# Tokens routed into two expert regions on chip, in place of every expert over all tokens

## The chip, the cores and the metric

One core of a Trainium2 chip runs the kernel. Its engines work side by side, each through its own queue in program order: TensorE (PE in the profile, its weight loads PEld), VectorE (DVE), ScalarE (ACT), GpSimd (POOL) and SyncE (SP), the last only to issue transfers. The metric is the device time of one execution in microseconds.

## The reference

Linear attention over 8 batches, 8 heads, 576 positions and head size 64, followed by a mixture of experts over the 4608 tokens of 512 numbers that come out of it. Each token goes to one of eight experts (512 to 1024 to 512); a bias that depends on the token's modality (0 or 1) is added to the router's logits.

```python
q_s = np.exp(q - q.max(-1));  q_s /= q_s.sum(-1) + 1e-09      # softmax over the 64 numbers of a head
k_s = np.exp(k - k.max(2));   k_s /= k_s.sum(2) + 1e-09       # softmax over the 576 positions
kv  = np.einsum('bhsd,bhse->bhde', k_s, v)
x   = np.einsum('bhsd,bhde->bhse', q_s, kv)                   # to 4608 x 512
logits = x @ w_gate + modality_bias[modality_id]
e_idx  = np.argmax(logits, axis=1);  gate_w = softmax(logits)[arange(N), e_idx]
for e in range(E):
    mask = e_idx == e
    out[mask] = gate_w[mask, None] * (np.maximum(x[mask] @ w1[e], 0.0) @ w2[e])
```

On the inputs as the reference draws them, routing gives 2277 tokens to one expert, 2331 to another and none to the other six; the two are those with the largest bias of modality 0 and of modality 1.

## The kernel before, in words

Attention runs in four rounds of two batches (`bp`). A round loads q, k and v (`q_m`, `k_m`, `v_mb` for the first 512 positions, `q_t`, `k_t`, `v_tb` for the last 64), exponentiates on ACT, divides q by its sums on POOL (L198), and builds `kv_ps` on PE (L222 with a column of ones, L230, for the sums of k). A normalised `kvn` gives, after a transpose (L258, copied by L260), the router's matrix `gmat`; q is transposed on PE (L277, copied by L285 into `qt_all`), from which come the logits (L293) and the attention output (L304, L320), copied to `xt_nat`: all 4608 tokens, bf16, with the 512 numbers on the partitions.

Then the routing, over all tokens at once (L346 to L421): the largest logit per token as a mask `eq_all`, the gate `gate_all`, and a list `r_ints` of those experts that have any token, with their number.

Then the FFN. `run_slot` loads the weights of one listed expert (L470, L483; cast to bf16 by POOL and DVE, L479, L492), and `expert_pass` runs it over all 36 tiles of 128 tokens, nine blocks of 512: L510 is the first layer, L520 and L524 the relu, L531 the second layer. L539 and L547 multiply by mask and gate and add into `y_tot`. The first expert runs always, the second under a condition on the number of experts, others in a loop of L581 that counts up to that number. Behind the loop, 40 transfers on POOL write `y_tot`, cast to f32 (L586).

A tile framework sets the order of instructions on each engine when the kernel is built, from the order of the code and priorities; on the chip each queue runs in that order, with semaphores between them.

Of the kernel before, what the change touches and what calls it, by code (L numbers as in the profile page):

```python
# [13 lines left out]
I32 = mybir.dt.int32  # L14
# [18 lines left out]
def kernel(  # L33
# [13 lines left out]
    P = 128  # L47

# [17 lines left out]

    mod_i32_all = _dram_bitcast(moe_modality_id, I32)

    const_pool = ctx.enter_context(tc.tile_pool(name="const", bufs=1))
    persist_pool = ctx.enter_context(tc.tile_pool(name="persist", bufs=1))  # L70

    ident = const_pool.tile([P, P], BF16)
    make_identity(nc, ident)

    ones_bf = const_pool.tile([P, P], BF16)
    nc.vector.memset(ones_bf, 1.0)

    wg_f32 = const_pool.tile([P, KD, E], FP32)
    nc.sync.dma_start(out=wg_f32, in_=moe_w_gate.rearrange("(kp p) e -> p kp e", p=P))
    wg_sb = const_pool.tile([P, KD, E], BF16)  # L80
    nc.vector.tensor_copy(out=wg_sb, in_=wg_f32)

    bias0 = const_pool.tile([P, E], FP32)
    bias1 = const_pool.tile([P, E], FP32)
    nc.sync.dma_start(out=bias0, in_=moe_modality_bias[0:1, :].to_broadcast([P, E]))
    nc.sync.dma_start(out=bias1, in_=moe_modality_bias[1:2, :].to_broadcast([P, E]))
    biasd = const_pool.tile([P, E], FP32)
    nc.vector.tensor_sub(out=biasd, in0=bias1, in1=bias0)


    mod_i32 = const_pool.tile([P, NBP, CPB, 2], I32)
    for bp in range(NBP):
        for bl in range(2):
            base = 2 * (1152 * bp + 576 * bl)
            nc.sync.dma_start(
                out=mod_i32[:, bp, 4 * bl : 4 * bl + 4, :],
                in_=bass.AP(tensor=mod_i32_all.tensor, offset=base, ap=[[8, P], [2, JW], [1, 2]]),
            )
        nc.sync.dma_start(
            out=mod_i32[0:64, bp, 8, :],  # L100
            in_=bass.AP(tensor=mod_i32_all.tensor, offset=2 * (1152 * bp + SMAIN), ap=[[2, 64], [1, 2]]),
        )
        nc.sync.dma_start(
            out=mod_i32[64:128, bp, 8, :],
            in_=bass.AP(tensor=mod_i32_all.tensor, offset=2 * (1152 * bp + 576 + SMAIN), ap=[[2, 64], [1, 2]]),
        )
    mod_f32 = const_pool.tile([P, NBP * CPB], FP32)
    nc.vector.tensor_copy(out=mod_f32, in_=mod_i32[:, :, :, 0].rearrange("p a b -> p (a b)"))

    xtn_pool = ctx.enter_context(tc.tile_pool(name="xtn", bufs=1, side="right"))  # L110
    xt_nat = xtn_pool.tile([P, KD, N], BF16)
    logits_all = persist_pool.tile([P, NT, E], FP32)

    r_ints = persist_pool.tile([1, 4 * E], I32)
    gate_all = persist_pool.tile([P, NT], FP32)
    eq_all = persist_pool.tile([P, NT, E], BF16)

    with (
        tc.tile_pool(name="qkv_stage", bufs=1) as stage_pool,
        tc.tile_pool(name="attn_sb", bufs=2) as asb_pool,  # L120
        tc.tile_pool(name="attn_small", bufs=2) as asm_pool,
        tc.tile_pool(name="kv_ps", bufs=2, space=bass.MemoryType.PSUM) as kvps_pool,
        tc.tile_pool(name="qt_ps", bufs=2, space=bass.MemoryType.PSUM) as qtps_pool,
        tc.tile_pool(name="x_ps", bufs=2, space=bass.MemoryType.PSUM) as xps_pool,
        tc.tile_pool(name="lg_ps", bufs=1, space=bass.MemoryType.PSUM) as lgps_pool,
        tc.tile_pool(name="tmp_ps", bufs=1, space=bass.MemoryType.PSUM) as tmpps_pool,
    ):
        for bp in range(NBP):
            b0 = 2 * bp
            q_m = stage_pool.tile([P, 2, H, JW, Dh], FP32, name="q_m")  # L130
            q_t = stage_pool.tile([P, H, Dh], FP32, name="q_t")
            k_m = stage_pool.tile([P, 2, H, JW, Dh], FP32, name="k_m")
            k_t = stage_pool.tile([P, H, Dh], FP32, name="k_t")

            def load_main(dst, src_t, b, bl, eng):
                eng.dma_start(
                    out=dst[:, bl],
                    in_=bass.AP(
                        tensor=src_t.tensor,
                        offset=src_t.offset + b * H * S * Dh,  # L140
                        ap=[[JW * Dh, P], [S * Dh, H], [1, JW * Dh]],
                    ),
                )

            def load_tail(dst, src_t, b, p0, eng):
                eng.dma_start(
                    out=dst[p0 : p0 + STAIL],
                    in_=src_t[b, :, SMAIN:S, :].transpose([1, 0, 2]),
                )

            for bl in range(2):
                b = b0 + bl
                load_main(q_m, q, b, bl, nc.sync)
                load_main(k_m, k, b, bl, nc.scalar)
                load_tail(q_t, q, b, 64 * bl, nc.scalar)
                load_tail(k_t, k, b, 64 * bl, nc.sync)

            eq_m = asb_pool.tile([P, 2, H, JW, Dh], BF16, name="eq_m")
            eq_t = asb_pool.tile([P, H, Dh], BF16, name="eq_t")
            ek_m = asb_pool.tile([P, 2, H, JW, Dh], BF16, name="ek_m")  # L160
            ek_t = asb_pool.tile([P, H, Dh], BF16, name="ek_t")
            v_mb = asb_pool.tile([P, 2, H, JW, Dh], BF16, name="v_mb")
            v_tb = asb_pool.tile([P, H, Dh], BF16, name="v_tb")

            for bl in range(2):
                b = b0 + bl
                nc.gpsimd.dma_start(
                    out=v_mb[:, bl],
                    in_=bass.AP(
                        tensor=v.tensor,  # L170
                        offset=v.offset + b * H * S * Dh,
                        ap=[[JW * Dh, P], [S * Dh, H], [1, JW * Dh]],
                    ),
                )
                nc.gpsimd.dma_start(
                    out=v_tb[64 * bl : 64 * bl + STAIL],
                    in_=v[b, :, SMAIN:S, :].transpose([1, 0, 2]),
                )
# [438 lines left out]
```

## Time and profile before

| | us |
|---|---|
| median of 3 runs | 476.06 (475.25 to 476.24) |
| span of the profiled execution, first to last instruction | 475.0 |
| PE busy | 358.5 |
| DVE busy | 200.3 |
| ACT busy | 115.4 |
| POOL busy | 76.8 |

Only the span of the profiled execution is given, not a time of its own with what lies around the span. A row of a stretch gives its start and end, its length, then for PE, PEld, DVE, ACT and POOL the busy time and the number of instructions, the clock that the throttle granted to PE, the busy share of the transfer engines and GB/s. A row of a group gives line, engine, operation, output and inputs, shapes and count, then the busy time of all and the mean nanoseconds of one, then the engine's idle time ahead of them and what ended it. Matmuls overlap, so the mean of one is longer than the distance between two.

### The profile page before, as it was taken

The numbers are of one execution on the slowest core, as the hardware profiler recorded it, in microseconds if no ns is written. First come the engines' busy times: TensorE is split into PE (matmuls) and PEld (weight loads), VectorE is DVE, ScalarE is ACT, GpSimd is POOL, SyncE is SP. The second block draws the span as 40 slices with busy tenths as digits, with TensorE's granted clock in tenths as the row PEclk, the third lists the DMA queues.
The fourth block names the chain that finished last, engine by engine and source line by source line (L and its number), as shares of the span: only waits on it lengthen the run. The fifth ranks groups of instructions, "written<-read, shape, count | busy, mean of one in ns | idle before, by whom it ended". The sixth has DMA issues, their size and how long they took to land. (4 is left out here: it accounts for less than half of the span.)

```text
span 475.0 us, 5993 instructions
## 1 busy us (share of the span) xinstructions
PE 358.5 (75%) x2404; PEld 190.0 (40%) x2404; DVE 200.3 (42%) x387; ACT 115.4 (24%) x227; POOL 76.8 (16%) x83
## 2 busy tenths in 40 slices
PE   0005956978854952899999999989999999999400
PEld 0005734847544720344444444434444444444100
DVE  1015573574576672343444444454433444433200
ACT  0434741753742220211112221112221111222000
POOL 5004324233015002400000000001000000000385
PEclk9999999999999999999999999999999999999955
DMA  9999596098000007600000000051000000000499
GB/s 159 219 281 301 88 295 159 9 256 236 1 1 1 2 1 268 220 1 1 0 1 0 1 0 0 1 177 46 0 0 2 0 1 0 1 1 0 105 393 303
DMA packets 48977, 41.93 MB, mean 88 GB/s; under 512 B 16688, under 2 KB 41264, under 8 KB 48944
## 3 DMA queue, kind: packets, MB, share of 16 engines
q0 software_dynamic: 17792, 14.16, 15.8%
q1 hardware_dynamic: 16880, 13.70, 10.3%
q10 hardware_dynamic: 14272, 13.63, 9.8%
q8 instruction: 21, 0.34, 0.3%
q14 instruction: 12, 0.10, 0.1%
HBM read 36.76 MB, written 9.44 MB: 97 GB/s over the span
## 5 line engine op out<-in xcount | busy, mean ns | idle before, releaser
L510 PE MATMUL h_ps<-xt_nat,w_sb 128*128 128x512 bf16 x576 | 131.2, 385 | 16.4 <-POOL w_sb L479 12.9
L531 PE MATMUL y_ps<-w_sb,hT 128*128 128x512 bf16 x576 | 129.0, 379 | 0.0
L520 ACT ACTIVATE hT<-h_ps 128x512 bf16<-128x512 f32 x72 | 43.0, 597 | 220.6 <-PE h_ps L510 123.3
L510 PEld LDWEIGHTS <-w_sb 128*128 128x128 bf16 x576 | 56.7, 99 | 87.9 <-POOL w_sb L479 14.3
L531 PEld LDWEIGHTS <-hT 128*128 128x128 bf16 x576 | 54.9, 98 | 70.8 <-DVE hT L524 4.0
L524 DVE TENSOR_SCALAR hT<-h_ps 128x512 bf16<-128x512 f32 x72 | 49.7, 692 | 76.5 <-ACT hT L520 42.6
L222 PE MATMUL kv_ps<-v_mb,ek_m 128*64 128x64 bf16 x256 | 37.4, 245 | 21.4 <-ACT ek_m L182 17.9
L586 POOL DMA_DIRECT2D out_dram<-y_tot x40 | 21.5, 544 | 124.4 <-issue 123.3
L539 DVE TENSOR_SCALAR y_tot<-y_ps,m_s 128x512 bf16<-128x512 f32 x36 | 27.0, 751 | 33.0 <-PE y_ps L531 33.0
L547 DVE SCALAR_TENSOR_TENSOR y_tot<-y_ps,m_s,y_tot 128x512 bf16<-128x512 f32 x36 | 27.0, 751 | 32.8 <-PE y_ps L531 32.8
L222 PEld LDWEIGHTS <-ek_m 128*64 128x64 bf16 x256 | 30.0, 152 | 23.3 <-ACT ek_m L182 17.9
L230 PE MATMUL kv_ps<-ones_bf,ek_m 128*64 128x1 bf16 x256 | 33.3, 193 | 0.0
L198 POOL TENSOR_TENSOR eq_m<-eq_m,qi_m 128x4096 bf16<-128x4096 bf16 x4 | 28.2, 7050 | 30.4 <-DVE ksum_inv L241 12.4
L230 PEld LDWEIGHTS <-ek_m 128*64 128x64 bf16 x256 | 30.5, 156 | 2.7 <-issue 2.6
L222 PE MATMUL kv_ps<-v_tb,ek_t 64*64 64x64 bf16 x64 | 15.4, 256 | 18.9 <-ACT ek_t L184 18.9
L277 PE MATMUL qt_ps<-ident,eq_m 128*64 128x128 bf16 x256 | 23.4, 313 | 8.0 <-POOL eq_m L198 7.3
L285 DVE CAST qt_all<-qt_ps 128x512 bf16<-128x512 f32 x36 | 24.4, 689 | 5.8 <-PE qt_ps L277 4.8
L492 POOL CAST w_sb<-w2st 128x512 bf16<-128x512 f32 x8 | 5.0, 627 | 125.9 <-DMA w2st<-in_moe_w_dram 125.8
L304 PE MATMUL xt_ps<-qt_all,kvn 128*128 128x512 bf16 x32 | 19.1, 596 | 6.2 <-ACT xt_nat L313 3.9
L277 PEld LDWEIGHTS <-eq_m 128*64 128x64 bf16 x256 | 14.8, 157 | 12.1 <-POOL eq_m L198 8.2
L188 DVE TENSOR_REDUCE qs_m<-eq_m 128x64 f32<-128x4096 bf16 x4 | 17.6, 4412 | 2.8 <-ACT eq_m L181 2.8
L181 ACT ACTIVATE eq_m<-q_m 128x2048 bf16<-128x2048 f32 x8 | 15.3, 1909 | 8.9 <-DMA q_m<-in_q_dram 8.8
(84 smaller groups left out, 237.0 us busy)
## 6 DMA issues: line engine op xcount, KB each, us to landing
k_m<-in_k_dram ACTq DMA_DIRECT2D x8, 1024.0 KB, 9.6
q_m<-in_q_dram SPq DMA_DIRECT2D x8, 1024.0 KB, 12.3
out_dram<-y_tot POOLq DMA_DIRECT2D x32, 256.0 KB, 4.2
v_mb<-in_v_dram POOLq DMA_DIRECT2D x8, 512.0 KB, 10.1
w1st<-in_moe_w_dram ACTq DMA_DIRECT2D x4, 512.0 KB, 4.4
w1st<-in_moe_w_dram SPq DMA_DIRECT2D x4, 512.0 KB, 5.4
w2st<-in_moe_w_dram ACTq DMA_DIRECT2D x8, 256.0 KB, 4.6
w2st<-in_moe_w_dram SPq DMA_DIRECT2D x8, 256.0 KB, 4.3
```

The costliest lines, as they stand in the source:

```text
L198: nc.gpsimd.tensor_tensor(out=eq_m, in0=eq_m, in1=qim_b, op=ALU.mult)
L222: nc.tensor.matmul(out=kv_ps[rows, 0:Dh], lhsT=lhsT, rhs=rhs, start=(si == 0), stop=False, skip_group_check=True,)
L230: nc.tensor.matmul(out=kv_ps[rows, Dh : Dh + 1], lhsT=lhsT, rhs=one_col, start=False, stop=(si == len(srcs) - 1), skip_group_check=True,)
L277: nc.tensor.matmul(out=qt_ps[64 * he : 64 * he + 64, pr, :], lhsT=tin, rhs=ident, start=True, stop=True, skip_group_check=True,)
L285: nc.vector.tensor_copy(out=qt_all[:, :, gc, :], in_=qt_ps)
L510: nc.tensor.matmul(out=h_ps[:, fj, :], lhsT=w1_sb[slot][:, kd, fglob * P : (fglob + 1) * P], rhs=xt_nat[:, kd, col0 : col0 + 4 * P], start ...
L520: nc.scalar.activation(out=hT[:, fglob, :], in_=h_ps[:, fj, :], func=ACT.Relu)
L524: nc.vector.tensor_scalar_max(out=hT[:, fglob, :], in0=h_ps[:, fj, :], scalar1=0.0)
L531: nc.tensor.matmul(out=y_ps, lhsT=hT[:, kf, t * P : (t + 1) * P], rhs=w2_sb[slot][:, kf, :], start=(kf == 0), stop=(kf == KF - 1),)
L539: nc.vector.tensor_scalar(out=y_tot[:, gt, :], in0=y_ps, scalar1=m_s[:, gt : gt + 1], scalar2=None, op0=ALU.mult,)
L547: nc.vector.scalar_tensor_tensor(out=y_tot[:, gt, :], in0=y_ps, scalar=m_s[:, gt : gt + 1], in1=y_tot[:, gt, :], op0=ALU.mult, op1=ALU.add,)
L586: nc.gpsimd.dma_start(out=dst_ap, in_=y_tot[rows, i, :])
```

## The change

The kernel is written anew. Attention goes batch by batch. The softmax sums of q come out of the same matmul as the logits (`gx` has two columns of ones), and those of k out of the kv matmul. Every batch is routed at once: each token that goes to the first expert (`key[0]`) gets the next free column from the left of `xs` (4864 columns), every other the next from the right. Per tile of 128 tokens, a 0/1 matrix `perm` sorts the tile on PE while it is transposed (`xT_ps`), and the whole tile is copied to both sides, at offsets `av` that ACT and DVE load into registers; what is wrong of a copy is written over by the next tile. The gate and q's sum are multiplied in on the way (`scl`, `x_sb`). The token numbers of the columns are gathered by another matmul (`id_ps`, `lst`) into an index list `idx`.

The FFN runs over columns: the left half with the first expert's weights, the right half with the second's, each in passes of 512, 512, 512, 512 and 384 columns. After every second batch one pass of each side follows (`ph`), after the last batch two of each. A tile's output is scattered to its rows of `out` by an indirect transfer on POOL; columns without a token have an index out of bounds and are not written. At the end a check of the counts (`ok`) sets the number of rounds of a loop, 0 or 8, which runs the FFN of every expert over all columns. Batches have priority over FFN passes in the order (`AHEAD`). All loads go through five staging buffers and SP.

```diff
-        for bp in range(NBP):
-            b0 = 2 * bp
...
-            nc.gpsimd.tensor_tensor(out=eq_m, in0=eq_m, in1=qim_b, op=ALU.mult)
...
-            run_slot(0, 0, True)
-            with tc.If(nact_r > 1):
-                run_slot(1, 1, False)
-            with tc.For_i(2, nact_r) as kx:
-                run_slot(kx, 0, False)
...
+    CAP = 2432
+    NSLOT = 2 * CAP
+    passes_a = [(min(i, NPH - 1), GW * i, min(GW, CAP - GW * i)) for i in range(5)]
+    passes_b = [(ph, NSLOT - lo - w, w) for ph, lo, w in passes_a]
...
+    stage = ctx.enter_context(tc.tile_pool(name="stage", bufs=5))
+    ybuf = ctx.enter_context(tc.tile_pool(name="ybuf", bufs=4))
+    mm = ctx.enter_context(tc.tile_pool(name="mm", bufs=3, space=bass.MemoryType.PSUM))
+    ff = ctx.enter_context(tc.tile_pool(name="ff", bufs=3, space=bass.MemoryType.PSUM))
...
+        nc.scalar.activation(out=view(ek, [[Dh, HG], [HG * Dh, NJ], [1, Dh]]), in_=kst, func=ACT.Exp)
+        nc.scalar.activation(out=view(eq, [[Dh, HG], [HG * Dh, NJ], [1, Dh]]), in_=qst, func=ACT.Exp)
...
+                    nc.tensor.matmul(
+                        out=kv[hg][:, 130 * hp : 130 * hp + 129],
+                        lhsT=ek[rows, j, P * hp : P * hp + P],
+                        rhs=vb[rows, j, hp, 0:129],
...
+        nc.scalar.copy(out=kvT, in_=kvT_ps[:, 0 : NP * P])
...
+        nc.vector.tensor_tensor(
+            out=lw,
...
+        nc.vector.tensor_copy(out=aoff_i[:, o : o + NT], in_=aoff[0:1, o : o + NT])
...
+        for t in range(NT):
+            nc.vector.tensor_scalar(
+                out=perm[:, t, :], in0=iota_row, scalar1=pos[:, t : t + 1], scalar2=None, op0=ALU.is_equal
+            )
...
+        _, av = nc.values_load_multi_w_load_instructions(
+            aoff_i[0:1, o : o + NT],
+            engines=[ENG.Activation, ENG.DVE],
...
+            nc.vector.tensor_tensor(
+                out=x_sb[0:T],
+                in0=view(x_ps, [[Dh, H], [1, Dh]], 0, (0, T)),
+                in1=view(scl, [[1, H], [0, Dh]], t * H, (0, T)),
+                op=ALU.mult,
+            )
...
+            wa = nc.scalar.copy(out=window(a, passes_a[ph], T, ph == NPH - 1), in_=xT_ps[:, :, 0:T])
+            wb = nc.vector.tensor_copy(
+                out=window(a + right, passes_b[ph], T, ph == NPH - 1, True), in_=xT_ps[:, :, 0:T]
+            )
...
+    def ffn(lo, w, slot, ix):
...
+            if f % 4 < 3:
+                nc.scalar.activation(out=hT[:, f, 0:w], in_=h_ps[:, 0:w], func=ACT.Relu)
+            else:
+                nc.vector.tensor_scalar_max(out=hT[:, f, 0:w], in0=h_ps[:, 0:w], scalar1=0.0)
...
+            if t % 4 < 3:
+                nc.vector.tensor_copy(out=y_sb, in_=y_ps)
+            else:
+                nc.scalar.copy(out=y_sb, in_=y_ps)
...
+            nc.gpsimd.indirect_dma_start(
+                out=out,
+                out_offset=bass.IndirectOffsetOnAxis(ap=ix[:, c : c + 1], axis=0),
+                in_=y_sb,
...
+    AHEAD = 4000
+    for b in range(B):
+        with tc.high_priority(offset=AHEAD):
+            stage_a(b)
+            stage_b(b)
+            if b == 0:
+                load_weights(eids[0], 0, (nc.scalar, nc.vector))
+                load_batch(2)
...
+        if b % 2:
+            ph = b // 2
+            idb, ab, sel = places()
...
+            for slot, (_, lo, w) in todo:
+                ffn(lo, w, slot, idx)
...
+    nr = nc.values_load(nrest[0:1, 0:1], min_val=0, max_val=E, skip_runtime_bounds_check_because=WHY)
+    with tc.For_i(0, nr) as e:
```

The order on PE before, where attention ends and the FFN begins (`tot_ps` counts the tokens of each expert, `h_ps` is the first layer):

```order
L369 LDWEIGHTS ones_bf
L369 MATMUL tot_ps<-eq_all,ones_bf 1x8
L304 LDWEIGHTS kvn
L304 MATMUL xt_ps<-qt_all,kvn 128x512
L320 LDWEIGHTS kvn
L320 MATMUL xt_ps<-qt_all,kvn 128x64
L510 LDWEIGHTS w_sb_2166
L510 MATMUL h_ps<-xt_nat,w_sb_2166 128x512
```

All of attention stands ahead of the first matmul of the FFN. The order on PE now, in batch 4 (`r_ps` ranks the tokens, `y_ps` is the second layer):

```order
L554 LDWEIGHTS W
L554 MATMUL h_ps<-xs,W 128x512
L386 LDWEIGHTS tri
L386 MATMUL r_ps<-isa,tri 128x5
L387 LDWEIGHTS ones
L387 MATMUL r_ps<-isa,ones 128x5
L568 LDWEIGHTS hT
L568 MATMUL y_ps<-W,hT 128x512
```

FFN of the tokens of batches 0 to 3 now stands between the steps of batch 4. This is so in batches 4 to 7. The passes that follow batch 1 stand as one piece between batches 1 and 2, with only the kv matmuls of batch 2 inside them, and the passes after batch 7 stand alone.

The order on DVE before, within an attention round:

```order
L260 COPY kvnT_sb<-kvnT_ps 128x128
L202 MEMSET kvn 128x512
L335 TENSOR_REDUCE logits_all<-lg_ps 128x72
L238 TENSOR_SCALAR kv_ps<-kv_ps 128x1
L285 CAST qt_all<-qt_ps 128x4x128
L241 RECIPROCAL ksum_inv<-kv_ps 128x1
```

The order on DVE now, in batch 3 (`lg` are the logits, `mx` their largest, `kk` the expert as a key, `isa` whether it is the first expert):

```order
L359 TENSOR_SCALAR qi<-lg_ps 128x40
L360 RECIPROCAL qi<-qi 128x40
L362 TENSOR_TENSOR lw<-lg_ps,qi 128x320
L369 TENSOR_REDUCE lg<-lw 128x40
L370 TENSOR_TENSOR lg<-lg,bsel 128x40
L372 TENSOR_REDUCE mx<-lg 128x5
L375 TENSOR_TENSOR eqm<-lg,mx 128x40
L376 TENSOR_TENSOR lg<-lg,mx 128x40
L378 TENSOR_TENSOR eqm<-eqm,wrow 128x40
L380 TENSOR_REDUCE kk<-eqm 128x5
L390 TENSOR_REDUCE gsum<-lg 128x5
L382 SCALAR_TENSOR_TENSOR isa<-kk,key,valid 128x5
```

Routing, which stood once behind attention, now stands in every batch, ahead of the tiles. The order on ACT before, in an attention round (`eq_m` is the exponential of q):

```order
L331 ACTIVATE xt_nat<-xt_ps 128x64
L248 ACTIVATE kvn<-kv_ps,ksum_inv 64x64
L263 ACTIVATE gmat<-g_ps 128x8
L181 ACTIVATE eq_m<-q_m 128x2048
L242 ACTIVATE kvn<-kv_ps,ksum_inv 64x64
```

The order on ACT now, where the first pair of passes ends (the `y_sb` row is the last tile of the second pass) and batch 2 goes on:

```order
L284 ACTIVATE ek<-st 128x4x9x64
L579 COPY y_sb<-y_ps 128x512
L285 ACTIVATE eq<-st 128x4x9x64 x2
L318 COPY et_180<-tp_ps 128x4x256
L318 COPY et_180<-tp_ps 128x4x64
L339 COPY kvT<-kvT_ps 128x512
L284 ACTIVATE ek<-st 128x4x9x64
L377 ACTIVATE lg<-lg 128x40
L467 TENSOR_LOAD aoff_i
```

The exponentials of q for batches 2 and 3 stand behind that copy and ahead of the copies of batch 2's transposed q.

More of the change, by code (lines that the diff above doesn't have):

```diff
@@ L75 @@
[L75 to L86, printed above, removed]
@@ L107 @@
[L107 to L128, printed above, removed]
-            b0 = 2 * bp
[L130 to L137, printed above, removed]
@@ L158 @@
[L158 to L168, printed above, removed]
+                        tensor=src.tensor,
@@ new lines @@
+    mraw = const.tile([P, B, NJ, 2], I32)
+    m32 = _dram_bitcast(moe_modality_id, I32)
+    for hg in range(2):
+        nc.scalar.dma_start(
+            out=mraw[64 * hg : 64 * hg + 64],
+            in_=bass.AP(tensor=m32.tensor, offset=m32.offset, ap=[[2 * NJ, 64], [2 * S, B], [1, 2 * NJ]]),
+        )
+    load_batch(0)
+    ident = const.tile([P, P], BF16)
+    make_identity(nc, ident)
+    ones = const.tile([P, P], BF16)
+    nc.vector.memset(ones, 1.0)
+    tri = const.tile([P, P], BF16)
@@ L455 @@
[L455 to L471 removed]
+                        tensor=moe_w1.tensor,
```

920 lines of the change are left out of this document (486 added, 434 removed).

## Prediction

> **What bounds the kernel now.** I read the page first: span, the busy line of the engines, the transfer rate by slice and the HBM bytes.
>
> ```profile
> span 475.0 us, 5993 instructions
> PE 358.5 (75%) x2404; PEld 190.0 (40%) x2404; DVE 200.3 (42%) x387; ACT 115.4 (24%) x227; POOL 76.8 (16%) x83
> GB/s 159 219 281 301 88 295 159 9 256 236 1 1 1 2 1 268 220 1 1 0 1 0 1 0 0 1 177 46 0 0 2 0 1 0 1 1 0 105 393 303
> HBM read 36.76 MB, written 9.44 MB: 97 GB/s over the span
> ```
>
> The shares are means over unlike stages, so the second view is the busy time by stretch: loading, attention, first expert weights, FFN, output.
>
> ```profile
> 0.00:18.00 18.00, 0.10 (x2) 0.10 (x3) 1.50 (x6) 3.20 (x3) 7.12 (x14) 1.00 1.10 182
> 18.00:180.00 162.00, 104.59 (x1252) 78.25 (x1252) 89.36 (x224) 69.17 (x152) 38.98 (x17) 1.00 0.57 127
> 180.00:188.00 8.00, 1.46 (x3) 0.28 (x3) 1.39 (x2) 0.00 (x0) 1.66 (x2) 1.00 0.92 346
> 188.00:446.00 258.00, 252.39 (x1149) 111.33 (x1149) 108.08 (x155) 43.01 (x72) 7.63 (x11) 1.00 0.07 23
> 446.00:475.00 29.00, 0.00 (x0) 0.00 (x0) 0.00 (x0) 0.00 (x0) 21.45 (x40) 0.56 1.23 327
> ```
>
> The five stretches run one after another. Attention (162 us) fills no engine; the FFN (258 us) fills PE; the output (29 us) is transfers alone. The profiled 475.0 us is 1.1 below the median of the runs, 476.06; I work in spans and add 1 at the end.
>
> The third view gives durations: PE streams, the cost of a PE start after idling, and DVE chains of small operations (timeline rows: start, length, operation).
>
> ```profile
> 88.50 0.61 PE L304 MATMUL xt_ps<-qt_all,kvn 128*128 128x512 bf16 x1
> 96.22 0.54 PE L293 MATMUL lg_ps<-gmat,qt_all 128*128 128x8 bf16 x13
> 188.58 5.30 PE L510 MATMUL h_ps<-xt_nat,w_sb 128*128 128x512 bf16 x13 [1.14 <-POOL w_sb L479]
> 319.34 3.41 PE L510 MATMUL h_ps<-xt_nat,w_sb 128*128 128x512 bf16 x15 [1.67 <-DVE w_sb L479]
> 439.81 4.70 PE L531 MATMUL y_ps<-w_sb,hT 128*128 128x512 bf16 x21
> 177.41 0.21 DVE L412 TENSOR_TENSOR sel_t<-rank,eidx_row 1x64 f32<-1x64 f32 x1
> 177.66 0.21 DVE L414 TENSOR_TENSOR sel_t<-sel_t,af 1x64 f32<-1x64 f32 x1
> 178.39 0.16 DVE L420 CAST r_ints<-idx_of_rank 1x8 int32<-1x8 f32 x1
> 179.31 0.21 DVE L573 TENSOR_TENSOR m_s<-eq_all,gate_all 128x36 f32<-128x36 f32 x1 [0.76 <-DVE r_ints L420]
> ```
>
> The group rows give engine durations, and the last two the output and load transfers.
>
> ```profile
> L510 PE MATMUL h_ps<-xt_nat,w_sb 128*128 128x512 bf16 x576 | 131.2, 385 | 16.4 <-POOL w_sb L479 12.9 <-DVE hT L524 1.8 <-DVE w_sb L479 1.7
> L520 ACT ACTIVATE hT<-h_ps 128x512 bf16<-128x512 f32 x72 | 43.0, 597 | 220.6 <-PE h_ps L510 123.3 <-DVE hT L524 97.4
> L317 DVE CAST xt_nat<-xt_ps 128x512 bf16<-128x512 f32 x16 | 11.0, 689 | 5.0 <-PE xt_ps L304 3.5 <-PE xt_ps L320 1.3 <-PE g_ps L262 0.2
> L329 DVE CAST xt_nat<-xt_ps 128x64 bf16<-128x64 f32 x16 | 3.5, 221 | 4.7 <-PE xt_ps L320 4.5 <-PE g_ps L262 0.2
> L260 DVE COPY kvnT_sb<-kvnT_ps 128x128 bf16<-128x128 bf16 x32 | 7.0, 219 | 3.6 <-PE kvnT_ps L258 3.6
> L350 DVE TENSOR_TENSOR lg<-logits_all,bias 128x288 f32<-128x288 f32 x1 | 0.4, 448 | 0.0
> L181 ACT ACTIVATE eq_m<-q_m 128x2048 bf16<-128x2048 f32 x8 | 15.3, 1909 | 8.9 <-DMA q_m<-in_q_dram 8.8
> L479 POOL CAST w_sb<-w1st 128x1024 bf16<-128x1024 f32 x4 | 4.3, 1088 | 40.4 <-DMA w1st<-in_moe_w_dram 40.4
> L479 DVE CAST w_sb<-w1st 128x1024 bf16<-128x1024 f32 x4 | 2.7, 689 | 6.7 <-DMA w1st<-in_moe_w_dram 6.7
> L586 POOL DMA_DIRECT2D out_dram<-y_tot x40 | 21.5, 544 | 124.4 <-issue 123.3 <-DMA out_dram<-y_tot 0.4
> out_dram<-y_tot POOLq DMA_DIRECT2D x32, 256.0 KB, 4.2
> ```
>
> **The change part by part.** *FFN once per token.* A streamed 512-column matmul costs (4.70 - 0.38) / 20 = 0.216 us. Now there are 8 passes of 512 columns and 2 of 384: first layer 8 x 32 x 0.216 + 2 x 32 x 0.162 = 65.7 us, second 38 x 8 x 0.216 = 65.7, together 131 in place of 1152 x 0.216 = 249: minus 118 us of PE, and with the idle that goes with it 258 - 131 = 127 off the path, if PE streams. A pass of 512 is 13.8 us, a pair 27.7, one of 384 10.4.
>
> *Output.* The 29 us at the end become 38 scatters, one behind each 128-row tile, so all but the last lie under later FFN. What stays is a copy (0.69), one scatter, its landing (4.2) and the exit from the fallback loop (about 2): 8. The scatter's cost on POOL is not in the trace. Bounds: 0.54 as the plain output, and 3.5, where four would take as long as a pass. I take 1.5, nearer the plain row, since it too makes a descriptor per row. At 3.5 POOL starts to pace.
>
> *Attention loads.* All on SP, five staging buffers. The bytes (36.8 MB) take 106 us at the 346 GB/s of the weight stretch and 202 at the 182 of the first; the last batch is wanted after 200 us, so I count nothing. If that cover goes, the next batch's k is late, and the exponential on ACT holds what stands behind it. The first 3.54 MB take 10 to 19 us; DVE's first chain I start at 18.5 (14 to 24).
>
> *PE in attention.* Per batch 98 matmuls of about 128 columns and 31 tiny ones. The row at 188.58 shows 13 matmuls after an idle stretch at (5.30 - 0.38) / 12 = 0.41 us, twice the price, though the granted clock there reads 1.00; at 319.34, after 1.67 us of idle, 15 take 0.216 each. L304 (0.61 against the 0.385 mean of L510) shows that attention ran at the slow price. So 128 columns cost 0.054 to 0.103, a tiny one (0.54 - 0.17) / 12 = 0.031: 6 to 11 us a batch. The Trainium skill, "TensorE: Matmul & The Clock Gate", Part 1, has the rule for this: after an idle window of some 3.4 us the array falls to half rate and needs such a window of work to recover; the trace agrees in the two rows, but its clock column does not show it. By that rule the attention of batches 0 to 3, whose short bursts are parted by DVE's chain, stays slow; by the fast row each of them would lose about 1 us of its waits, 4 in the sum.
>
> *DVE in attention, the new bound.* A PSUM operand of n columns costs 0.154 + n x 1.04 ns (221 at 64, 689 at 512), half the slope in bf16 (219 at 128). Per batch: five x_sb 3.45; five xs copies 3.18; et 0.68; four kvbd 1.15; lw and its sum 0.98 (as L350); hhi, hlo, lst 1.44; 34 small ones at 0.19 (a dependent one follows after 0.25, 177.41 to 177.66, a free one after less) 6.5; one register load 0.76 (row at 179.31). Sum 18.1 us, 145 for eight, where DVE was busy 89 in the whole of attention.
>
> DVE also waits, since the chain crosses engines: for kv (36 matmuls, 2.2); for et on ACT (about 1.0, by 597 for 512) and kvT (0.6) and g (0.4) behind them, 2.4 after DVE's own copy; lg 0.9; r 0.4; x and xT 1.0; slow PE 0.7: 7.6. A batch with nothing beside it: 26 us. The next batch's kv stands behind the last x_ps, so batches barely overlap.
>
> *Sum along the order of the queues.* Start 18.5. Batch 0: 26. Batch 1: 29 (two weight casts on DVE, 1.22 each by L479, and places). First pair of passes alone on PE: 27.7 + kv 2.2 + slow start 2.5 = 32.5. Batch 2: 26 (kv is done, 3 less; but the exponentials of q for batches 2 and 3, 2.1 each by L181, stand on ACT behind the last y copy, 3 more). Batch 3: 26.5. Batches 4 and 5 with the second pair of passes: DVE has 2 x 18.1 + 4 relus and 6 copies at 0.69 = 43, PE 13 to 22 + 27.7; walking the order by hand, the copies fill about half of the waits: 55 (51 if all hide, 60 if none). Batches 6 and 7: 55. Last passes: 27.7 + 20.8 + 2.5 = 51. End 8. Together 327.5, reported 328. Both ends: with no waits at all 18.5 + 21 + 24 + 30 + 22 + 22 + 2 x 46 + 49 + 7 = 285; with start 24, waits of 11 a batch and pairs of 63, 24 + 29 + 33 + 33 + 30 + 30 + 126 + 52 + 10 = 367.
>
> *Waits that are added.* The register load on DVE and on ACT holds, on each, the xs copies of that batch, and through the PSUM buffers the next x_ps on PE; its 0.76 on DVE is in the 18.1, ACT has room. SP's register load of the expert numbers stands ahead of the weights and of all loads from batch 2 on; it waits for DVE's set-up, which ends before the five buffers first come free. That set-up (two memsets of 2432 words, 2.5 each by the slope above, and some 40 small ones, 13 us in all) lies beside the first load of 10 to 19 us; with a load of 10 it would cost up to 3, inside the bounds of the start. On ACT the exponentials wait for loads, and behind them in the queue stand et and kvT, for which PE and then DVE wait: this is where a late load would show first.
>
> *POOL.* v casts 2 x 1.22 and hv about 1 a batch (L479's rate), 28 us beside 38 scatters: hidden; without that cover, kv waits for v.
>
> **The rivals.** *A, the queues overlap better:* free small operations pair up, and kv of the next batch comes early. For it: the independent small DVE rows follow each other faster than their length. Against it: one batch's chain is dependent, and three PSUM buffers are shared. With half the waits gone: about 290.
>
> *B, slow PE in the mixed stages:* if the idle gaps there keep the array at 0.41, a pair of passes costs 52 in place of 27.7, PE has 22 + 52 = 74 a pair and 80 with its waits, 25 more each: 378. For it: L304. Against: gaps between FFN pieces are mostly under 3.5 us, and a gap of 1.67 cost nothing. By the skill's page a gap under its window does nothing, so the page is on my side here.
>
> *C, slower than before: scatters pace the kernel.* POOL could start scattering at about 78 us; 28 us of casts and 38 scatters end at 475 from 9.7 us each. For it: nothing in the trace shows an indexed transfer. Against: the plain one takes 0.54. At 12 us: 78 + 28 + 456 = 562.
>
> *D, the fallback runs.* The check asks 512 to 640 tokens of the first expert after two batches, 1024 to 1280 after four, 1536 to 1920 after six; routing the given inputs by the reference gives 572, 1119, 1690, and 2277 and 2331 in the regions of 2432. If it ran nevertheless: eight experts of 131 + about 15 of weights, 1170 more: 1500.
>
> **How the numbers follow.** Forecast 0.62 (its own range 305 to 350); A 0.20; B 0.14; C 0.02; D 0.01; the rest, no difference, 0.01. The range takes in A and B but for their far ends: 285 to 372. 0.2% is about what a measurement here can tell from none; faster 0.96, same 0.01, slower 0.03.
>
> **What would show it.** Right: DVE 210 to 225 us busy; 608 FFN matmuls' worth of PE at 0.216; batches 2 and 3 at 24 to 28 us each with PE under half busy; a last stretch of about 51 us of full PE; scatters at 1 to 2 us. Wrong: POOL as releaser of kv or of y_sb, ACT waiting for k or q, FFN matmuls at 0.41 between attention pieces, or a batch period beside 26.

## The result, and the profile after

The changed kernel takes 345.55 us (median of 4 runs, 343.94 to 346.28) where the kernel before took 476.14 in the same session: a ratio of 0.7255, 95% interval 0.7234 to 0.7275. The forecast was 328 (285 to 372). It was 17.5 too low, and more than that lies in three places of the profile, which other terms partly pay back. In the table of the experiments, the median of f1_fillers leaves out one execution of four, which ran 1.6% above the fastest at a lower clock.

The page of the profiled execution (346.28 us): span, busy time of the engines, then PE's busy share and the granted clock in 40 slices of 8.6 us.

```profile
span 344.6 us, 4646 instructions
PE 219.9 (64%) x1637; PEld 126.0 (37%) x1657; DVE 174.6 (51%) x558; ACT 116.2 (34%) x161; POOL 75.7 (22%) x86
PE   0033373369994041572699997499799599999900
PEclk9999999999999555555589999569999969999985
```

Three things are to be seen: two slices with PE at 0 and 4 in the middle of the work, right behind the first full stretch; a clock near 5 in the five slices behind them; two empty slices at the end.

The same by stage, cut at the terms of the forecast. A batch begins with `kinv`, the reciprocal of k's sums, the first thing DVE makes of it (that of batch 2, at 83.67, lies inside the first pair, so the row of batch 2 begins where the pair ends). The rows are batch 0, batch 1, first pair of passes, batch 2, batch 3, batches 4 and 5 with passes, 6 and 7 with passes, last passes, end. Columns: start and end, length, busy PE, PEld, DVE, ACT, POOL, then clock, transfer share, GB/s.

```profile
26.20:49.40 23.20, 11.08 (x120) 8.79 (x121) 15.10 (x57) 8.21 (x10) 3.89 (x3) 1.00 0.93 271
49.40:74.75 25.35, 9.81 (x96) 7.51 (x95) 18.86 (x64) 10.84 (x13) 3.84 (x3) 1.00 0.80 202
74.75:106.95 32.20, 31.32 (x160) 13.96 (x163) 10.73 (x19) 13.03 (x16) 2.53 (x3) 1.00 0.76 198
106.95:148.70 41.75, 11.85 (x126) 9.39 (x126) 14.73 (x47) 10.76 (x12) 11.62 (x11) 0.55 0.75 177
148.70:172.85 24.15, 13.17 (x133) 10.12 (x133) 16.83 (x62) 10.68 (x13) 4.68 (x4) 0.50 0.98 195
172.85:226.30 53.45, 46.10 (x382) 26.06 (x386) 37.90 (x125) 25.49 (x37) 14.91 (x14) 0.88 0.48 116
226.30:276.04 49.74, 42.30 (x345) 23.39 (x351) 36.09 (x121) 17.43 (x32) 9.12 (x8) 0.95 0.09 33
276.04:327.10 51.06, 50.79 (x235) 24.09 (x240) 13.79 (x24) 14.23 (x26) 13.17 (x14) 0.95 0.16 61
327.10:344.60 17.50, 0.17 (x2) 0.00 (x0) 1.03 (x4) 0.00 (x0) 2.39 (x3) 0.66 0.10 37
```

| stage | forecast | measured | difference |
|---|---|---|---|
| start, to the first `kinv` | 18.5 | 26.2 | +7.7 |
| batch 0 | 26 | 23.2 | -2.8 |
| batch 1 | 29 | 25.4 | -3.6 |
| first pair of passes | 32.5 | 32.2 | -0.3 |
| batch 2 | 26 | 41.8 | +15.8 |
| batch 3 | 26.5 | 24.1 | -2.4 |
| two pairs with batches 4 to 7 | 110 | 103.2 | -6.8 |
| last passes | 51 | 51.1 | +0.1 |
| end | 8 | 17.5 | +9.5 |

Batch 2, the largest, is read from the timeline (start, length, operation; in brackets the engine's idle time ahead and what ended it), and from the group of the scatters (busy, mean ns of one, idle).

```profile
88.43 1.19 POOL L581 DMA_INDIRECT out_dram<-y_sb,idx  x1 [19.71 <-DVE y_sb L577]
96.98 0.97 POOL L581 DMA_INDIRECT out_dram<-y_sb,idx  x1 [7.36 <-DMA out_dram<-y_sb,idx]
106.57 0.97 POOL L581 DMA_INDIRECT out_dram<-y_sb,idx  x1 [8.62 <-DMA out_dram<-y_sb,idx]
116.29 0.97 POOL L581 DMA_INDIRECT out_dram<-y_sb,idx  x1 [8.75 <-DMA out_dram<-y_sb,idx]
122.49 0.97 POOL L581 DMA_INDIRECT out_dram<-y_sb,idx  x1 [5.23 <-DMA out_dram<-y_sb,idx]
125.98 0.97 POOL L581 DMA_INDIRECT out_dram<-y_sb,idx  x1 [2.52 <-DMA out_dram<-y_sb,idx]
...
121.82 0.59 ACT L579 COPY y_sb<-y_ps 128x512 f32<-128x512 f32 x1 [19.99 <-DMA out_dram<-y_sb,idx]
122.30 4.14 ACT L285 ACTIVATE eq<-st 128x2304 bf16<-128x2304 f32 x2
...
124.48 2.10 PE L308 MATMUL tp_ps<-ident,eq 128*128 128x128 bf16 x18 [17.53 <-ACT eq L285]
```

```profile
L581 POOL DMA_INDIRECT out_dram<-y_sb,idx x38 | 37.3, 983 | 138.9 <-DMA out_dram<-y_sb,idx 61.0
```

A scatter costs POOL 0.98 us, but each begins only when the one before it has landed: all write the same `out`, and the order of the program makes the second write wait for the first. Beside the loads the first four scatters come 8.6 to 9.7 us apart, later ones 3.49 (122.49 to 125.98). The four `y_sb` buffers are then full, so the last y copy of the pair waits 20 on ACT. Behind it in ACT's queue stand both exponentials of q, and PE's transposes wait for these: 17.53 idle.

At the end the same series runs late, and the loop that does no turn follows:

```profile
329.73 0.97 POOL L581 DMA_INDIRECT out_dram<-y_sb,idx  x1 [2.19 <-DVEq L655]
333.85 0.97 POOL L581 DMA_INDIRECT out_dram<-y_sb,idx  x1 [3.15 <-DMA out_dram<-y_sb,idx]
```

At the start DVE had its set-up ahead of `kinv` and stood in it, waiting for the modality numbers (issued on ACT's queue, not on SP), while kv had been done at 19.15:

```profile
14.66 0.18 DVE L183 CAST modf<-mraw 64x32 f32<-64x32 int32 x1 [6.54 <-DMA mraw<-in_moe_modality_id_dram]
20.13 0.18 DVE L183 CAST modf<-mraw 64x32 f32<-64x32 int32 x1 [5.29 <-DMA mraw<-in_moe_modality_id_dram]
22.26 2.08 DVE L237 MEMSET xs<- 128x2432 f32 x1 [0.46 <-issue]
26.25 0.21 DVE L322 TENSOR_SCALAR kinv<-kv_ps 128x2 f32<-128x2 f32 x2
...
16.90 2.25 PE L296 MATMUL kv_ps<-vb,ek 64*128 64x129 bf16 x36 [16.90 <-POOL vb L287]
```

### The profile page after: what moved, and what is told of

Read it like the earlier page. It is cut to its first block, busy times and chain, and to the rows that moved or that the text cites. A ratio compares the mean times of both kernels' runs of the same rounds, so it can differ in the third digit from the quotient of the medians.

```text
span 344.6 us, 4646 instructions
## 1 busy us (share of the span) xinstructions
PE 219.9 (64%) x1637; PEld 126.0 (37%) x1657; DVE 174.6 (51%) x558; ACT 116.2 (34%) x161; POOL 75.7 (22%) x86
## 4 chain that ended last, share of the span: by engine, by line
PE 16%; DMA 13%; issue 13%; DVE 6%; POOL 2%; ACT 1%; POOLq 0%; ACTq 0%
DMA out_dram<-y_sb,idx 13%; PE y_ps L568 5%; PE h_ps L554 4%; PE kv_ps L296 2%; PE xT_ps L494 2%; POOL hv L438 1%; DVE x_sb L486 1%; PE x_ps L478 1%; PE tp_ps L308 1%; PE id_ps L521 1%; ACT ek L284 1%; POOL out_dram L581 0%; PE lg_ps L350 0%; DVE hT L564 0%; DVE y_sb L577 0%
## 5 line engine op out<-in xcount | busy, mean ns | idle before, releaser
L554 PE MATMUL h_ps<-xs,W 128*128 128x512 bf16 (+1 forms) x307 | 76.8, 394 | 3.2 <-ACT xs L504 1.5
L568 PE MATMUL y_ps<-W,hT 128*128 128x512 bf16 x297 | 68.3, 379 | 1.3 <-DVE lo L428 0.7
L581 POOL DMA_INDIRECT out_dram<-y_sb,idx x38 | 37.3, 983 | 138.9 <-DMA out_dram<-y_sb,idx 61.0
L504 ACT CAST xs<-xT_ps 128x512 f32 (+2 forms) x40 | 21.9, 547 | 79.7 <-PE xT_ps L494 76.1
L562 ACT ACTIVATE hT<-h_ps 128x512 bf16<-128x512 f32 (+1 forms) x60 | 34.2, 578 | 39.1 <-PE h_ps L554 31.4
L554 PEld LDWEIGHTS <-W 128*128 128x128 bf16 x320 | 31.8, 103 | 35.7 <-issue 11.2
L568 PEld LDWEIGHTS <-hT 128*128 128x128 bf16 x304 | 29.1, 98 | 33.6 <-DVE hT L564 0.6
L486 DVE TENSOR_TENSOR x_sb<-x_ps,scl 128x512 bf16<-128x512 f32 (+1 forms) x40 | 27.4, 686 | 11.0 <-PE x_ps L478 10.8
L308 PE MATMUL tp_ps<-ident,eq 128*128 128x128 bf16 x144 | 15.5, 282 | 26.2 <-ACT eq L285 21.7
L296 PE MATMUL kv_ps<-vb,ek 64*128 64x129 bf16 x288 | 18.5, 271 | 16.9 <-POOL vb L287 16.9
L505 DVE CAST xs<-xT_ps 128x512 f32 (+2 forms) x40 | 25.3, 633 | 4.9 <-ACT xs L504 4.6
L478 PE MATMUL x_ps<-kvbd,et 128*128 128x128 bf16 (+1 forms) x160 | 20.9, 271 | 2.7 <-ACT et L318 2.7
L579 ACT COPY y_sb<-y_ps 128x512 f32<-128x512 f32 x8 | 4.7, 588 | 41.1 <-PE y_ps L568 21.1
## 6 DMA issues: line engine op xcount, KB each, us to landing
st<-in_v_dram SPq DMA_DIRECT2D x16, 576.0 KB, 10.8
```

The costliest lines, as they stand in the source:

```text
L296: nc.tensor.matmul(out=kv[hg][:, 130 * hp : 130 * hp + 129], lhsT=ek[rows, j, P * hp : P * hp + P], rhs=vb[rows, j, hp, 0:129], start=(j = ...
L308: nc.tensor.transpose(out=view(tp, [[2 * nj * 64, 2], [1, 64]], hp * nj * 64 + jj * 64), in_=eq[:, c0 + jj, P * hp : P * hp + P], identity ...
L478: nc.tensor.matmul(out=x_ps[0:T, P * p_ : P * p_ + P], lhsT=et[:, p_, tcol[t] : tcol[t] + T], rhs=kvbd[:, p_, :], start=True, stop=True,)
L486: nc.vector.tensor_tensor(out=x_sb[0:T], in0=view(x_ps, [[Dh, H], [1, Dh]], 0, (0, T)), in1=view(scl, [[1, H], [0, Dh]], t * H, (0, T)), o ...
L504: wa = nc.scalar.copy(out=window(a, passes_a[ph], T, ph == NPH - 1), in_=xT_ps[:, :, 0:T])
L505: wb = nc.vector.tensor_copy(out=window(a + right, passes_b[ph], T, ph == NPH - 1, True), in_=xT_ps[:, :, 0:T])
```

## The experiments

| run | on top of | median us | change | ratio to the kernel before, 95% |
|---|---|---|---|---|
| e1_scatter_free | changed kernel | 326.29 | -19.3 | 0.6849 to 0.6872 |
| e2_bias_behind | changed kernel | 345.53 | 0.0 | 0.7188 to 0.7274 |
| e3_no_loop | changed kernel | 338.99 | -6.6 | 0.7107 to 0.7131 |
| e4_passes_last | changed kernel | 427.16 | +81.6 | 0.8957 to 0.9006 |
| f1_fillers | e1 | 319.44 | -6.9 | 0.6694 to 0.6723 |
| f2_hlo_thrice | e1 | 339.90 | +13.6 | 0.7134 to 0.7162 |
| f3_hv_on_dve | e1 | 328.79 | +2.5 | 0.6887 to 0.6921 |
| f4_passes_last | e1 | 369.85 | +43.6 | 0.7748 to 0.7784 |
| h1_order_alone | e1 | 306.09 | -20.2 | 0.6421 to 0.6448 |
| g1_relu_to_act | e1 | 321.52 | -4.8 | 0.6715 to 0.6770 |
| g2_order_fill | f1 | 308.54 | -10.9 | 0.6453 to 0.6524 |
| g3_all | e1, with e2, g1 and g2 | 293.01 | -33.3 | 0.6128 to 0.6177 |

**The series of scatters.** Two scatters never write the same row of `out`, so the wait can go by naming the target apart.

```diff
-                out=out,
+                out=bass.AP(tensor=out.tensor, offset=out.offset, ap=out.ap,
+                            dep_tracking_offset=out.offset + c * N * D),
```

> One edit: each scatter's target is entered in the dependence tracking as rows of its own, so a scatter no longer waits until the one before it has landed. Theory (scatters in series by landing: 8.6 to 9 us apart beside the load stream, 3.49 apart alone; through four y buffers they hold the y copies, behind the last y copy on ACT the exponential of q of batch 2, and so PE for 17.5): batch 2 falls from 41.8 to 25 to 28, the end from 17.5 to 9 to 12, together 345.6 - 15 - 7 = 324 (320 to 329). Rival 1, batch 2 is late because of its own load of q or a slow PE and the series only stands beside it: under 5 gained, above 340. Rival 2, scatters side by side take the transfers from the load stream: batch 2 falls by under 8 and later batches wait for loads, 332 to 340.

Measured 326.29. Stages of this run, batch 2 and the end, and two scatters of the second pass:

```profile
107.00:133.70 26.70, 11.89 (x127) 9.40 (x128) 13.47 (x47) 10.54 (x12) 7.12 (x6) 0.55 1.04 251
311.00:323.50 12.50, 0.00 (x0) 0.00 (x0) 0.30 (x3) 0.00 (x0) 0.97 (x1) 0.64 0.13 47
```

```profile
102.39 0.97 POOL L581 DMA_INDIRECT out_dram<-y_sb,idx  x1 [7.64 <-DVE y_sb L577]
104.12 0.97 POOL L581 DMA_INDIRECT out_dram<-y_sb,idx  x1 [0.76 <-DVE y_sb L577]
```

These scatters wait for their y copies and no longer for a landing. Batch 2 takes 26.7 (forecast 26) and the end 12.5. Rival 1 falls: the same load of q and the same clock of 0.55 are there. Rival 2 falls too, since batch 2 lost 15 and not under 8. The wait's chain is shown.

**The loop at the end.**

```diff
-    nr = nc.values_load(nrest[0:1, 0:1], min_val=0, max_val=E, skip_runtime_bounds_check_because=WHY)
-    with tc.For_i(0, nr) as e:
...
```

> The general loop behind the passes is left out (it does no turn with these inputs), with the register load ahead of it. Theory (SP's queue shows a wait of 4.9 at the end for PE's jump over the loop's body, behind the last landing): 345.6 - 5 = 340.6. Rival 1, the jump lies beside the last scatters' landing: 0 to -1. Rival 2, the loop's part that PE's instruction stream carries costs time earlier too: more than -8.

Measured 338.99, 6.6 less, between the theory and rival 2. The last scatter of this run:

```profile
331.54 0.97 POOL L581 DMA_INDIRECT out_dram<-y_sb,idx  x1 [2.52 <-DMA out_dram<-y_sb,idx]
```

From that start the end takes 5.5 here (331.54 to 337.0), 10.8 in the changed kernel (333.85 to 344.6): 5.3 is the exit, with its register load. The profiled executions differ by 7.6; of the 2.3 ahead of the last scatter, 1.3 stand already at `kinv` of batch 7 (251.15 for 252.46), and their cause stays open.

**The set-up at the start.**

```diff
-    for hg in range(2):
-        pr = (64 * hg, 64)
-        nc.vector.tensor_copy(
...
+        if b == 0:
+            bias_rows(kvbd_op)     # the same casts and rows, on DVE behind kvbd of batch 0
+        qi = small.tile([P, NT * H], FP32, name="qi")
```

> One edit: the three casts of the modality numbers and the two bias rows made from them stand on DVE behind kvbd of batch 0, in place of the set-up. Theory (DVE stood 5.3 and 6.5 for the modality numbers, that land 18 us late, and only then did 6 us of set-up, so kinv of batch 0 came at 26.25 though kv had ended at 19.15): kinv at 19.3, the et copy at 24.6, bound by q that lands at 21.1, in place of 27.95; the total falls by 3.3, to 342.3. Rival, the set-up is hidden behind q anyway or the rest of the DVE queue takes the gain back: within 1 of 345.6.

345.53, no gain: the rival is right. `kinv` came at 19.39 and the copy of the transposed q (`et`) at 24.61 as expected; where the 3.3 went is in the rows of DVE and POOL:

```profile
24.61 0.69 DVE L326 COPY et<-tp_ps 128x1024 bf16<-128x1024 bf16 x1 [1.89 <-PE tp_ps L318]
32.78 1.12 DVE L406 TENSOR_TENSOR scl<-qi,gsum 128x40 f32<-128x40 f32 x1
33.82 1.14 DVE L421 CAST aoff_i<-aoff 1x5 int32<-1x5 f32 x1
...
32.70 2.24 POOL L297 CAST vb<-st 128x1152 bf16<-128x1152 f32 x2 [14.54 <-DMA st<-in_v_dram]
...
132.53 2.86 DVE L394 SCALAR_TENSOR_TENSOR isa<-kk,key,valid 128x5 bf16<-128x5 f32 x1
...
133.13 2.24 POOL L297 CAST vb<-st 128x1152 bf16<-128x1152 f32 x2
```

`scl` took 1.12 (0.19 in the changed kernel) and `aoff_i` 1.14 (0.16), both while POOL cast v: 1.9 lost, and `kinv` of batch 1 was 1.3 ahead (47.96 for 49.27). That lead lasted to the routing of batch 2. There `isa` took 2.86 (0.23 in the changed kernel) and ended with POOL's cast of v (135.39 and 135.37), so batch 3 began only 0.14 ahead (148.58 for 148.72). In both places the earlier DVE work met casts that it had missed before.

**What the interleaving is worth.** First try, passes only written behind batch 7:

> All ten passes stand behind batch 7 in place of two behind every second batch. Theory by terms as measured: kinv 26.2, batches 0 and 1 48.6, six batches without passes at 24.1 = 144.6, ten passes 131 + 2.5, end 17.5: 370 (365 to 376); the interleaving is then worth 48 in the two mixed stages and gives 17 to 20 of them back in batch 2. Rival 1, the mixed stages hide little and the scatters' wait in batch 2 is all that counts: 340 or less. Rival 2, without passes between them the batches wait for their loads: above 380.

427.16, in the range of rival 2, but for one load only, and it answers another question. The order of writing does not set the order of the queues: the first pair still ran beside batch 2 (its scatters stood at the end), and half of q of batch 2 was issued behind k and v of batches 3 to 5; the batches behind took 25.1 each. Its waits between 105 and 165:

```profile
PE tp_ps L308 <- ACT eq L285: 35.0, 1, 35.0
...
ACT eq L285 <- DMA st<-in_q_dram: 26.1, 1, 26.1
```

Second try, every first product of a pass held behind the last xT of batch 7 and the loads in the order of writing:

```diff
-                ffn(lo, w, slot, idx)
+            late += todo                       # run behind batch 7
...
+                tc.add_manual_dep(
+                    w1.ins,
+                    last_xt[0].ins.name,
...
```

> On top of e1_scatter_free (326.3): all ten passes behind batch 7, every pass held behind the last xT of batch 7 on PE, and all loads in the order in which they are written. (In e4 PE still took the first two passes beside batch 2, and half of q of batch 2 stood on SP's queue behind the loads of batches 3 to 5, so ACT waited 26 for it; the batches behind took 25.1 each with nothing beside them.) Theory: first two batches end at 75, six more at 25.1, ten passes 131 + 2.5, end 13: 372 (366 to 378), so that beside attention four passes cost next to nothing, 46 to 50 in all. Rival 1, loads set the pace without passes between: above 385. Rival 2, the mixed stages hide little: 345 or less.

Measured 369.85 for 372. Two batches in the windows of this run, and the first and the last products of its passes in the timeline:

```profile
101.80:126.80 25.00, 11.73 (x128) 9.54 (x128) 17.18 (x61) 9.52 (x11) 3.93 (x3) 0.50 1.05 215
177.00:200.30 23.30, 12.22 (x131) 9.75 (x129) 15.43 (x54) 8.79 (x11) 1.65 (x1) 0.50 0.00 1
```

```profile
221.11 9.72 PE L571 MATMUL h_ps<-xs,W 128*128 128x512 bf16 x32
...
349.85 5.34 PE L591 MATMUL y_ps<-W,hT 128*128 128x512 bf16 x24
```

From `kinv` of batch 2 (76.85) to that of batch 7 (200.34) a batch alone takes 24.7, beside full transfers (25.0 at 1.05) and beside none (23.3); the ten passes take 134. Two batches beside a pair of passes take 53.5 and 49.7 in the changed kernel, two alone 49.4: the pair, 27.7 by itself, costs 0.3 to 4 there. Against e1 the interleaving is worth 43.6. But f4 also has its loads in order, which e1 has not; the run that differs from f4 only in where the passes stand is h1 below (306.09), and against it the interleaving is worth 63.8.

**Is DVE the bound of a batch?**

```diff
+        for _ in range(2):
+            hlo_again = sb.tile([P, NT, P], BF16, name="hlo_again", bufs=1)
+            nc.vector.tensor_tensor(
+                out=hlo_again, in0=view(iota_row, [[0, NT], [1, P]]), in1=view(lo, [[1, NT], [0, P]]), op=ALU.is_equal
+            )
```

> On top of e1_scatter_free (326.3): the one-hot hlo is made three times a batch, two of them into a tile that nobody reads; DVE gets 2 x 0.83 more a batch, 13.3 in all. Theory (DVE paces every batch, alone or with passes): +10 to +13, 336 to 340. Rival 1, DVE paces the batches that stand alone only and has slack beside the passes: +5 to +7, 331 to 333. Rival 2, hlo stands where DVE waits anyway: within 2 of 326.

+13.6. It is not quite the count that was expected: the added ones took more than 0.83.

```profile
L435 DVE TENSOR_TENSOR hlo_again<-iota_row,lo 128x640 bf16<-128x640 bf16 x16 | 20.6, 1287 | 0.0
```

```profile
154.25 1.65 POOL L443 TENSOR_TENSOR hv<-hhi,vals 128x570 bf16<-128x570 bf16 x1 [12.87 <-DVE hhi L439]
154.81 1.76 DVE L435 TENSOR_TENSOR hlo_again<-iota_row,lo 128x640 bf16<-128x640 bf16 x1
157.10 0.81 DVE L435 TENSOR_TENSOR hlo_again<-iota_row,lo 128x640 bf16<-128x640 bf16 x1
```

One that begins while POOL makes hv takes 1.76, one behind it 0.81. So 20.6 of DVE cost 13.6, two thirds. By `kinv` of batches 0, 4 and 7, batches 0 to 3 cost 8.8 for 10.3 that were added, and batches 4 to 6, beside passes, 4.1 for 7.7: DVE's queue sets the batches that stand alone, and the mixed ones only in part. That is nearer to rival 1 than its +5 to +7 lets it seem, since that range was worked out with 0.83 for each. The Trainium skill, "SBUF — State Buffer", section "SBUF: two separate sides", says that DVE and GpSimd share a pair of ports as an exclusive lock, which a DVE operation with two inputs from SBUF and a GpSimd operation can't hold together, the loser waiting for the whole instruction. The trace agrees: 154.25 + 1.65 = 155.90, and the held operation ended 0.67 behind that.

The other way round, hv from POOL to DVE:

```diff
-        nc.gpsimd.tensor_tensor(
+        nc.vector.tensor_tensor(
             out=hv,
```

> On top of e1_scatter_free (326.3): hv is made on DVE in place of POOL. Theory (PE waits 11 in all for POOL's hv, 1.6 each, in a queue that holds the next x_ps behind id_ps): the wait goes, DVE gets some 0.45 a batch, net -3 to -6: 320 to 323. Rival, DVE is the bound and the wait was beside DVE's chain: +3 to +5.

+2.5, the rival's side. hv takes 0.86 on DVE against 1.53 on POOL in e1, but PE's waits for it did not go away: 12.9 in all, where e1 has 8.3 (the 11 of the theory is the changed kernel's), since hv now stands behind other work in DVE's queue.

And work taken off DVE beside batches 4 to 7:

```diff
-            if f % 4 < 3:
+            if f % 4 < 3 or mixed:
...
-            if t % 4 < 3:
+            if t % 4 < (1 if mixed else 3):
```

> On top of e1_scatter_free (326.3): in the four passes beside batches 4 to 7, all relus and three of four y copies go to ACT in place of DVE (8 relus of 0.68 and 8 copies of 0.69 off DVE, 11.0 in all). Theory (DVE paces the mixed stages too; two added hlo per batch cost all of their 13.3): -8 to -11, 315 to 318. Rival 1, the work only changes queues: on ACT it stands ahead of the et, kvT and xs copies that PE waits for, and gives it back: within 3 of 326. Rival 2, the mixed stages are bound by PE: within 1 of 326.

-4.8, between the theory and rival 1. Taking 11 off DVE pays less than half; from `kinv` of batch 4 to that of batch 7 it took 78.5, in e1 78.7, and from there to the last product 69.8 for 73.7, so the gain came only behind `kinv` of batch 7. So in this order of the queues less work on DVE did not shorten batches 4 to 6, though more of it lengthened them in part (f2).

**The slow clock and the loads' order.** Fillers, held behind the matmul that stands ahead of each wait:

```diff
+            w = nc.tensor.matmul(out=w_ps, lhsT=ones, rhs=fill, start=True, stop=True)   # batches 0 to 3, in PE's waits
```

> On top of e1_scatter_free (326.3): in batches 0 to 3, matmuls of 512 columns whose result is never read fill PE's waits (14 behind the logits, 7 behind the rank matmuls, 3 behind each x_ps). Theory (the granted clock of 0.50 to 0.61 in these stretches is PE's idling, and its slow matmuls lie on the batch's chain: kv 2.66 against 1.20, 18 transposes 2.1 against 1.2, xT 0.61 against 0.40): the clock of these stretches rises to 0.9 or more and a batch gets 2 to 3 shorter: 314 to 318. Rival, the chain on DVE sets the batch and PE's slow matmuls lie beside it, while fillers stand ahead of matmuls that are wanted: 324 to 330, with a higher clock all the same.

319.44, 6.9 less, just short of the 314 to 318 of the theory. Rows of this run, batch 3 and kv of batch 3, and the wait in batch 2:

```profile
133.00:155.00 22.00, 17.63 (x167) 9.61 (x166) 16.26 (x63) 8.81 (x12) 3.90 (x3) 0.92 0.97 195
```

```profile
107.33 2.10 PE L321 MATMUL tp_ps<-ident,eq 128*128 128x128 bf16 x18 [5.06 <-ACT eq L298]
...
131.22 1.61 PE L309 MATMUL kv_ps<-vb,ek 64*128 64x129 bf16 x36
```

The Trainium skill, "TensorE: Matmul & The Clock Gate", Part 1, has it that an array with work keeps its full rate. The trace agrees: the clock rises from 0.50 to 0.92, and kv falls from 2.66 to 1.61. Batch 3 falls from 24.1 to 21.8, so slow PE cost it about 2.3. Batch 1, to its first pass, gained 1.7 and batch 0 only 0.3, where the 14 fillers still ran at the slow price (5.57) and held the rank matmuls. Batch 2 gave 3.4 back (53.8 from `kinv` of batch 2 to that of batch 3, for 50.4): its q came 2.4 earlier only where `kinv` stood 4.3 earlier, and the 14 fillers behind its logits took 5.76 at the slow price. Why q is late stands on SP's queue in the changed kernel: one half of q of batch 2 at 57.54, the other with the next q.

```profile
57.54 0.59 SPq L100 DMA_DIRECT2D st<-in_q_dram  x1
58.38 6.08 SPq L253 DMA_DIRECT2D st<-in_moe_w_dram  x2
...
95.04 1.92 SPq L100 DMA_DIRECT2D st<-in_q_dram  x3
```

Loads in order, and fewer fillers:

```diff
+                in_order(d)      # each load held behind the one written before it on SP
...
-            warm(14, op)
+            warm(9, op)
```

> On top of f1_fillers (319.9): the loads stand on SP in the order in which they are written (in f1 the second half of q of batch 2 stood behind the weights and behind k and v of batch 3, and PE waited 5.1 for its exponential), and 9 fillers in place of 14 stand behind the logits (14 took 5.76 at the slow price, over the wait of 3.6). Theory: -5 of the wait, -1 to -2 of the fillers: 313 to 315. Rival, the transfers are full in that stretch (DMA share 1.04), so the same bytes in another order make something else late, k or v of batch 3: 318 to 321.

308.54, more gain than expected. Which of the two edits did it is told by the order without fillers (the first line of the diff alone):

> On top of e1_scatter_free (326.3): the loads stand on SP in the order of writing, without fillers. In this order of the queues the transposes of batch 2 stand on PE between the second products of the first pass, where in e1 they stand behind both passes. Theory (the first pair of passes hides batch 2 as the later pairs hide theirs; kinv of batch 3 came 36 after that of batch 2 in g2 and 50.4 in e1): -13 to -15, 311 to 313, and the fillers are worth what is left to g2's 308.5, 3 to 5. Rival, g2's gain came from PE kept busy: within 3 of 326, or q still lands late and holds the passes that now stand behind its transposes: above 326.

306.09: the order alone is worth 20.2, more than the 13 to 15 expected, and beside it the fillers do not gain 3 to 5 but lose 2.4 (in g2, 27 of them stood ahead of the next x_ps at the end of batch 2, for 6.2). The row that shows it, first pair with batch 2 in one stretch, and the transposes of batch 2:

```profile
75.00:117.00 42.00, 36.85 (x286) 19.13 (x292) 24.86 (x67) 22.45 (x29) 12.43 (x11) 0.98 0.85 221
...
88.14 1.17 PE L323 MATMUL tp_ps<-ident,eq 128*128 128x128 bf16 x18
```

42.0 where e1 took 32.0 + 26.7. All of q of batch 2 is issued by 59.2, and in the order of the queues the framework set batch 2 between the pieces of the first pair, as it does with the later ones; in e1 the transposes stood behind both passes (109.76). The edit changed both, the load and PE's order, and no run separates them.

Last, the edits of e1, e2, g1 and g2 in one kernel:

> All edits that gained, together, the general loop kept: scatters free of each other, the bias rows behind kvbd of batch 0, loads in the order of writing, fillers as in g2, relus and y copies of the mixed stages on ACT as in g1. If the effects add: 326.3 - 12 (g2) - 9 (g1) - 1.3 = 304. If those of g1 or g2 fall to their rivals, 312 to 318.

293.01, 11 below the sum of the effects. From `kinv` of batch 4 to that of batch 7 it takes 67.9, in g2 80.4: off DVE the relus and copies pay here what they did not pay in g1. Why only here was not separated. It beats the changed kernel by 52.5; since fillers cost in g2, a version without them was the next to try and was not run.

## Why the prediction held, step by step

- *FFN once per token*: right. 0.216 per matmul, 32.2 for 32.5 and 51.06 for 51; f4's ten passes took 134 for 131 + 2.5.
- *Scatters*: the step that failed. "All but the last lie under later FFN", and 1.5 us with bounds up to 3.5, priced POOL's time alone, which is 0.98. The wait for the landing was missing. Rival C had scatters pacing the kernel, but by their cost on POOL, and asked for 9.7 for each of 38; the first three gaps were 8.6 to 9.7, the later ones about 3.5. One of the prediction's own signs of being wrong stood there: a batch period beside 26. The series cost 15 in batch 2 (41.8 for 26.7 in e1) and 5 of the end's 9.5, more than the whole miss of 17; e1 gave back 19.3.
- *End*: 8 was too small by e1 as well (12.5). "About 2" for the loop's exit measured 5.3 by e3, and e1 keeps the loop.
- *Start*: the bounds of 14 to 24 took the set-up as lying beside the load. The small transfers of modality numbers (36 KB each, issued by 3.2) landed at 14.6 and 20.1, beside the bulk loads, and DVE's queue stood for them: 26.2. Yet e2 shows that the term was not worth its 7.7, because q landed at 21.1 anyway.
- *DVE's batch*: 18.1 busy and 7.6 waiting; batch 3 shows 16.8 and 7.3, so the waits did not halve as rival A asked. For the batches alone the bound was named rightly (f2); for the mixed ones it holds only in part (f2, g1). The busy total, 174.6 for 210 to 225, was too high, and that range does not follow from the prediction's own terms, which add to about 195 (145, 50 relus and copies at 0.69, the set-up of 13 and two casts).
- *Slow PE, 0.7 a batch, 1 to be had by the fast row*: mis-sized; f1 shows 2.3 in batch 3, 1.7 in batch 1 and 0.3 in batch 0, where fillers stood in the way. Rival B's place was wrong: in the mixed stages FFN matmuls kept the fast price (18 in 4.04 at 184.30, 0.215 each), with a clock of 0.88 and 0.95.
- *Loads counted at nothing*: near the truth for their bytes (a batch of f4 took 25.0 beside full transfers and 23.3 beside none), but their order was worth 20.2 (h1, with the order on PE that came with it). It showed where the prediction had said a late load would show first, at the exponentials on ACT.
- *Mixed stages*: 55 each for 53.5 and 49.7, and by f4 a pair of passes adds 0.3 to 4 to two batches.

So 328 is near 345.55 partly by luck, because errors of +33 and -16 met. It is nearer to e1, 326.29, the same kernel without the series, where the start (26.7) and the end (12.5) are the terms left too small.

## What to carry to other kernels

Price an indexed write by what the next one waits for, not by what it costs the issuing engine: where several write one tensor, look whether the second waits for the landing of the first, and follow the buffers back from there. Read the order of the load queue against the order of need; with a half load that slipped behind others, a whole batch was not hidden here. And when an edit gains in one engine's queue and the time stays, look what the earlier instruction now runs beside.

## What was not expected of the hardware

- A scatter of 128 rows of 2 KB takes POOL 0.97, and lands 2.7 us after its issue (median). In the series the next one began 2.5 after the end of the one before when little else moved, and 7.4 to 8.8 after it beside the loads.
- Small DVE operations took 1.1 and 2.9 in place of 0.2 beside v casts on POOL, and an operation of 0.81 took 1.76 beside hv.
- The granted clock reads 1.00 up to 107 us in the changed kernel, though ahead of the first pass PE works at the slow price: 4 matmuls of xT took 0.61 at 69.77, as they do later at 0.50, and 0.40 in f1 with fillers, where the clock reads 1.00 as well.
- The exit from a loop that does no turn, with its register load, took 5.3 us (e3).
